# Loading k and v of a packed attention stage as four tokens to a partition, with the last 64 tokens of every head loaded apart

## The chip, the cores and the metric

The kernel runs on one core of one Trainium2 chip. The metric is the time of one execution on the device in microseconds. Before the change the median of 3 runs is 1391.37 us (1388.29 to 1396.19).

## What is computed

The reference is a packed attention followed by two gated feed-forward layers, all in float32:

```python
q, k, v: (8, 8, 576, 64)      # batch, heads, tokens, head_dim
p:       (8, 8, 32, 64)       # 32 packed queries per head

def sm_attn(qq, kk, vv):
    s = (1 / sqrt(64)) * qq @ kk.T
    a = exp(s - max(s)); a = a / (sum(a) + 1e-9)
    return a @ vv

P   = sm_attn(p, k, v)        # 32 x 64 per head, from 576 tokens
out = sm_attn(q, P, P)        # 576 x 64 per head, from 32 packed rows
x   = out as (4608, 512)
x   = (silu(x @ w_gate) * (x @ w_val)) @ w_out
x   = ((x @ w1) * (x @ w2)) @ w3 @ w_out2
```

The change concerns only the first line, the product of the packed queries p with k and v. The order of the 576 tokens is free there, as long as k's scores and v's rows use the same one: max, sum and the weighted sum run over all of them.

## The kernel before

**Units and steps.** The work on p, k and v goes in 16 units, one for each half batch entry (4 heads of 576 tokens); `u = 2 * b + Q`. A loop over steps `s` runs the units as a pipeline. In step `s` the program has, in this order: `pa_kT(s)` (turn k of unit s), the loads of v for unit s and of k for unit s + 4, `pa_s(s - 1)` (scores), `pa_PT(s - 4)` (turn the finished packed rows), `pa_T(s - 2)` (turn the attention weights), `pa_exp(s - 1)`, and `pa_P(s - 3)` (weights times v). Between them, at written-out steps and quarter steps, stand other tasks (`run(s, ...)`): the work on q for the first two batch entries (tables `QS`, `QD`), loads of raw weights (`RAW0`), their conversion on ACT and DVE (`WS`), and the first products of the feed-forward layer (`CS`, `S1`). Each engine takes its instructions in the order of the program text (`manual_schedule`). Behind the pipeline the feed-forward layers follow, which keep the tensor engine busy to the end of the kernel.

**Loads.** All loads stand in one queue, SP's. A unit has 576 KB of k and as much of v. `load_kv` issues for k one DMA into `km` (128 partitions, 18 tokens of one head in each, 4608 bytes in a row), and for v two DMAs into `vm` (96 partitions, 6 tokens of each of 4 heads: 1024 bytes in a row in the first DMA, 512 in the second). `km` and `vm` have four buffers each.

**Waits of the queue.** Every DMA waits for the eighth one ahead of it to land, since the program has eight semaphores for this queue in turn. A load of `km` for unit u also waits until `pa_kT(u - 4)` has read its buffer.

**The unit's work.** `pa_kT` turns p's tile (one PE transpose) and `km` (nine) into PSUM tiles `pkr` and `pk`, and ACT copies them to `kT` in two copies (L501, L502). `pa_s` has 8 matmuls of 64 rows by 32 columns into `psp`; DVE takes the maximum (L517, L518), ACT the exponential with its sum (L524). `pa_T` makes six transposes of 96 columns into `pat` (L536), and ACT copies them to `apT` (L540). `pa_P` has 24 matmuls of 96 rows by 32 columns and 64 moving columns (L550), accumulated over six groups of tokens, and DVE divides by the sum (L554).

**What the prediction's steps touch:** `load_p` L466, `load_kv` L472, `pa_kT` L489, `pa_s` L505, `pa_T` L530, `pa_P` L543, and the step loop at L604. The conversion of raw weights is `conv` at L332; its ACT part is L345, and stands in ACT's queue ahead of that step's copies.

Of the kernel before, what the change touches and what calls it, by code (L numbers as in the profile page):

```python
# [8 lines left out]
F32 = mybir.dt.float32  # L9
# [3 lines left out]
AF = mybir.ActivationFunctionType  # L13
# [4 lines left out]
KVB = 4  # L18
VB = 4
# [19 lines left out]
def packed_attention_moe_kernel(  # L39
# [24 lines left out]
    nc = tc.nc  # L64
    B, H, S, D = q.shape
# [3 lines left out]
    DF2 = w1.shape[1]  # L69
    HS = S // 2  # L70
    NR = S // 32
    NV = 6
    PK = S // NV
    NF = DFF // 128
    NB32 = S // 32
    ND = DM // 128
# [4 lines left out]
    scale = 1.0 / float(D) ** 0.5  # L81

    def pool(name, side, bufs=1, **kw):
        return tc.alloc_tile_pool(name=name, bufs=bufs, side=side, reuse_waits="tile", **kw)
# [21 lines left out]
    ident = const.tile([128, 128], F32, name="ident")  # L106
# [354 lines left out]
    pa = pool("pa", "left", bufs=2)  # L461

    kv = {}
    zp = pa.tile([128, B, 2, 2, 64], F32, tag="zp", name="zp", bufs=1)

    def load_p(b0, b1):  # L466
        nc.sync.dma_start(zp[:, b0:b1, :, 0], p[b0:b1].rearrange("b (q h) j d -> (h j) b q d", q=2))

    def twice_p(b0, b1):
        nc.gpsimd.tensor_copy(zp[:, b0:b1, :, 1], zp[:, b0:b1, :, 0])  # L470

    def load_kv(u, nm):  # L472
        if not 0 <= u < 2 * B:
            return
        b, Q = divmod(u, 2)
        src = {"k": k, "v": v}[nm]
        if nm == "k":
            m = pa.tile([128, NR, D], F32, tag="km", name=f"km{u}", bufs=KVB)
            nc.sync.dma_start(m, src[b, 4 * Q:4 * Q + 4].rearrange("h (p r) d -> (h p) r d", r=NR))
        else:  # L480
            m = pa.tile([PK, 4, NV, D], F32, tag="vm", name=f"vm{u}", bufs=VB)
            rows = src[b, 4 * Q:4 * Q + 4].rearrange("h (p r) d -> p h r d", r=NV)
            for r0, r1 in ((0, 4), (4, NV)):
                pin_at["sp"] = nc.sync.dma_start(m[:, :, r0:r1], rows[:, :, r0:r1])
        kv[nm, u] = m

    kT_t, ap_t, apT_t, sm_t, Pd_t = {}, {}, {}, {}, {}

    def pa_kT(u):  # L489
        km = kv.pop(("k", u))  # L490

        kT = pa.tile([128, NR // 2 + 1, 128], F32, tag="kT", name=f"kT{u}")
        b, Q = divmod(u, 2)
        t1 = psum1(f"pkr{u}")
        nc.tensor.transpose(t1[:, 128:256], zp[:, b, Q].rearrange("p e d -> p (e d)"), ident)
        t = psum(f"pk{u}")
        for m in range(NR // 2):
            nc.tensor.transpose(
                t[:, m // 4, 128 * (m % 4):128 * (m % 4) + 128] if m < 8 else t1[:, 0:128],
                km[:, 2 * m:2 * m + 2, :].rearrange("p r d -> p (r d)"), ident)  # L500
        nc.scalar.copy(kT[:, 0:8], t.rearrange("p a (m n) -> p (a m) n", n=128))  # L501
        nc.scalar.copy(kT[:, 8:10], t1[:, 0:256].rearrange("p (m n) -> p m n", n=128))  # L502
        kT_t[u] = kT

    def pa_s(u):  # L505


        kT = kT_t.pop(u)
        t = psum(f"psp{u}")
        for hq in range(4):  # L510
            for e in range(2):
                es = slice(64 * e, 64 * e + 64)
                nc.tensor.matmul(
                    t[hs[hq], e, 0:HS].rearrange("j (m p g) -> j g m p", m=3, g=3), lhsT=kT[es, 9, hs[hq]],
                    rhs=kT[es, 0:9, hs[hq]].rearrange("d (g m) p -> d g m p", g=3), start=True, stop=True, tile_position=(64 * e, 32 * hq))
        mx = pa.tile([128, 1], F32, tag="mx", name=f"mx{u}")
        nc.vector.reduce_max(mx, t[:, :, 0:HS], axis=AX.XY)  # L517
        nc.vector.tensor_scalar_mul(mx, mx, -scale)  # L518
        return t, mx

    def pa_exp(u, t, mx):
        a = pa.tile([128, NV, PK], F32, tag="ap", name=f"ap{u}")
        sm = pa.tile([128, 1], F32, tag="sm", name=f"sm{u}", bufs=3)
        nc.scalar.activation(  # L524
            a.rearrange("j (m e) p -> j e m p", e=2),
            t[:, :, 0:HS].rearrange("j e (m p) -> j e m p", p=PK),
            AF.Exp, bias=mx, scale=scale, accum_out=sm)
        ap_t[u], sm_t[u] = a, sm

    def pa_T(u):  # L530
        a, sm = ap_t.pop(u), sm_t[u]
        nc.vector.tensor_scalar(sm, sm, 1e-9, None, op0=ALU.add)
        nc.vector.reciprocal(sm, sm)
        t = psum(f"pat{u}")
        for r in range(NV):
            nc.tensor.transpose(  # L536
                t[:PK, r % 2, 128 * (r // 2):128 * (r // 2) + 128],
                a[:, r], ident)
        aT = pa.tile([PK, 2, 3, 128], F32, tag="apT", name=f"apT{u}")
        pin_at["act"] = nc.scalar.copy(aT, t[:PK, :, 0:384].rearrange("p e (m n) -> p e m n", m=3))  # L540
        apT_t[u] = aT

    def pa_P(u):  # L543
        vm = kv.pop(("v", u))
        aT = apT_t.pop(u)
        sm = sm_t.pop(u)
        t = psum1(f"pP{u}")
        for r in range(NV):
            for hq in range(4):
                nc.tensor.matmul(  # L550
                    t[hs[hq], 0:64], lhsT=aT[:, r % 2, r // 2, hs[hq]], rhs=vm[:, hq, r, :],
                    start=(r == 0), stop=(r == NV - 1), tile_position=(0, 32 * hq))
        Pd = pa.tile([128, 2, 64], F32, tag="Pd", name=f"Pd{u}")
        pin_at["dve"] = nc.vector.tensor_scalar(  # L554
            Pd, t[:, 0:64].rearrange("p (o d) -> p o d", o=1).to_broadcast([128, 2, 64]), sm, None, op0=ALU.mult)
        Pd_t[u] = Pd

    def pa_PT(u):
        t = psum1(f"pPT{u}")[:, 0:128]
        nc.tensor.transpose(t, Pd_t.pop(u).rearrange("p a b -> p (a b)"), ident)  # L560
        nc.scalar.copy(PTd[:, u], t)  # L561

    U = 2 * B
    load_p(0, 1)
# [32 lines left out]
    def run(s, slot):  # L597
        for at in [at for at in extra if s + slot <= at < s + slot + 0.25]:
            for fn, args in extra.pop(at):
                fn(*args)  # L600

    last = int(max(max(extra), U + 3))
    with tc.manual_schedule(engines=M0):
        for s in range(last + 1):  # L604
            if s < U:
                pa_kT(s)
            load_kv(s - VD, "v")
            load_kv(s + KVB, "k")
            run(s, 0)
            run(s, 0.25)  # L610
            if 0 <= s - 1 < U:
                x = pa_s(s - 1)
            if 0 <= s - 4 < U:
                pa_PT(s - 4)
            run(s, 0.5)
            if 0 <= s - 2 < U:
                pa_T(s - 2)
            if 0 <= s - 1 < U:
                pa_exp(s - 1, *x)
            if 0 <= s - 3 < U:  # L620
                pa_P(s - 3)
            run(s, 0.75)
# [466 lines left out]
```

## Time and profile before

| | |
|---|---|
| time, median of 3 runs | 1391.37 us (1388.29 to 1396.19) |
| span of the profiled execution | 1393.5 us (the profile gives no other time for it) |
| PE busy | 1351.7 us, 97% of the span |
| PE weight loads, DVE, ACT, POOL busy | 1240.4, 656.0, 574.4, 384.4 us |
| chain that ended last | PE 80% of the span |
| DMA queue of SP | 228.64 MB in 188752 packets, 55.2% of 16 DMA engines |
| granted TensorE clock, mean | 0.993 |

The profile is of one execution, and its 1393.5 us stand 2.1 us above the median of the runs and inside their spread. Busy shares over the whole span say little about the change, which lies in the first tenth of the kernel: the prediction reads the stretches there one by one. [...]

### The profile page before, as it was taken

The page shows a single profiled execution, that of the slowest core. Times are in us where ns is not written, and L with a number is a line of the kernel's source. Part 1 is how long each engine was busy: PE and PEld are TensorE (multiplying, and loading weights), DVE is VectorE, ACT ScalarE, POOL GpSimd, SP SyncE. Part 2 cuts the span into 40 slices and gives each one's busy share as a digit, 9 for nine tenths or more (in the row PEclk, how much of TensorE's full clock was granted, in tenths as well). Part 3 has the DMA queues.
Part 4 walks back from the last instruction along what each step waited for, and adds up shares of the span by engine and source line. Part 5 has one row for each costly group of instructions (what it writes and reads, how often), then busy time and mean ns, then how long its engine had stood idle before and what let it go on. Part 6 is the DMA issues. An engine that isn't in the chain of part 4 may idle for free.

```text
span 1393.5 us, 25570 instructions
## 1 busy us (share of the span) xinstructions
PE 1351.7 (97%) x10228; PEld 1240.4 (89%) x10228; DVE 656.0 (47%) x946; ACT 574.4 (41%) x940; POOL 384.4 (28%) x309
## 2 busy tenths in 40 slices
PE   7779999999999999999999989999999999999998
PEld 5558899999999999999888989989999899898997
DVE  3466668436464365553263377833423323234130
ACT  5575635336243463344554245533323233333231
POOL 0223223333323332253444225502112022021120
PEclk9899999999999999999999999999999999999999
DMA  9997667544355544135452148937638357285441
GB/s 272 251 236 200 217 189 240 169 120 107 117 127 169 159 122 142 51 117 159 125 151 87 61 132 289 330 112 223 193 115 253 131 175 237 70 251 174 133 155 46
DMA packets 188870, 230.27 MB, mean 165 GB/s; under 512 B 70736, under 2 KB 119888, under 8 KB 188752
## 3 DMA queue, kind: packets, MB, share of 16 engines
q1 hardware_dynamic: 188752, 228.64, 55.2%
q8 instruction: 81, 1.33, 0.4%
q14 instruction: 37, 0.30, 0.1%
HBM read 179.04 MB, written 49.55 MB: 164 GB/s over the span
## 4 chain that ended last, share of the span: by engine, by line
PE 80%; DVE 2%; POOL 2%; DMA 1%; issue 1%; ACT 1%; SPq 0%; DVEq 0%; POOLq 0%; ACTq 0%
PE px L653 19%; PE pA L962 14%; PE po L1026 14%; PE pg L440 9%; PE pv L440 8%; PE pB L962 7%; PE pC L962 3%; PE pc L408 3%; PE pw L717 2%; PE psq L205 1%; POOL ul L88 0%; DMA wo3r<-wo3d 0%; POOL wo2l L88 0%; DMA x2r<-X2d 0%; DVE x2T L787 0%
## 5 line engine op out<-in xcount | busy, mean ns | idle before, releaser
L88 POOL TENSOR_TENSOR ul<-u,uh 128x576 fp32r<-128x576 f32 x96 | 146.0, 1521 | 333.2 <-ACT uh L92 328.2
L982 POOL TENSOR_TENSOR c<-s,s 128x384 f32<-128x384 f32 x48 | 49.6, 1033 | 378.9 <-ACT s L977 378.1
L653 PE MATMUL px<-uh,woh 128*128 128x384 f32 x576 | 147.9, 337 | 2.4 <-DVE acc L663 1.4
L653 PE MATMUL px<-ul,woh 128*128 128x384 f32 x576 | 147.2, 336 | 2.6 <-POOL ul L88 2.6
L653 PE MATMUL px<-uh,wol 128*128 128x384 f32 x576 | 147.0, 336 | 0.0
L977 ACT COPY s<-pA 128x384 f32<-128x384 f32 x144 | 69.0, 479 | 183.1 <-PE pA L962 178.6
L449 DVE TENSOR_TENSOR u<-u,pv 128x576 f32<-128x576 f32 x96 | 71.8, 749 | 109.9 <-PE pv L440 96.9
L1026 PE MATMUL po<-wo_hi,abh 128*128 128x512 f32 x288 | 112.2, 389 | 1.0 <-ACT abh L92 1.0
L1026 PE MATMUL po<-wo_hi,abl 128*128 128x512 f32 x288 | 112.3, 390 | 0.3 <-DVE abl L88 0.3
L1026 PE MATMUL po<-wo_lo,abh 128*128 128x512 f32 x288 | 112.2, 389 | 0.0
L92 ACT CAST uh<-u 128x576 fp32r<-128x576 f32 x96 | 64.7, 674 | 115.2 <-DVE u L449 114.8
L663 DVE TENSOR_TENSOR acc<-acc,px 128x768 f32<-128x768 f32 x72 | 68.1, 948 | 92.2 <-PE px L653 92.0
L653 PEld LDWEIGHTS px<-uh,woh 128*128 128x128 f32 x576 | 103.4, 189 | 5.3 <-DVE acc L663 1.8
L653 PEld LDWEIGHTS px<-ul,woh 128*128 128x128 f32 x576 | 104.5, 188 | 3.1 <-POOL ul L88 3.1
L653 PEld LDWEIGHTS px<-uh,wol 128*128 128x128 f32 x576 | 104.6, 189 | 0.0
L88 DVE TENSOR_TENSOR abl<-ab,abh 128x768 fp32r<-128x768 f32 x48 | 47.0, 980 | 104.5 <-ACT abh L92 104.4
L88 POOL TENSOR_TENSOR wol<-wof,woh 128x512 fp32r<-128x512 f32 x48 | 63.4, 1334 | 107.3 <-ACT woh L92 101.3
L440 PE MATMUL pg<-aTh,ch 128*128 128x288 f32 x384 | 87.1, 308 | 1.2 <-ACT u L445 1.2
L445 ACT ACTIVATE u<-pg 128x576 f32<-128x576 f32 x96 | 62.4, 651 | 59.8 <-PE pg L440 58.2
L440 PE MATMUL pv<-aTh,ch 128*128 128x288 f32 x384 | 82.9, 297 | 2.2 <-ACT PTd L561 1.5
L440 PE MATMUL pg<-aTh,cl 128*128 128x288 f32 x384 | 82.4, 296 | 0.0
L440 PE MATMUL pv<-aTl,ch 128*128 128x288 f32 x384 | 82.1, 295 | 0.0
(305 smaller groups left out, 3107.1 us busy)
## 6 DMA issues: line engine op xcount, KB each, us to landing
ws<-wsd SPq DMA_DIRECT2D x245, 256.0 KB, 3.1
wf<-Wd SPq DMA_DIRECT2D x36, 512.0 KB, 5.0
wsd<-ws SPq DMA_DIRECT2D x49, 256.0 KB, 3.0
km<-in_k_dram SPq DMA_DIRECT2D x16, 576.0 KB, 13.3
wof<-wod SPq DMA_DIRECT2D x36, 256.0 KB, 3.0
x2r<-X2d SPq DMA_DIRECT2D x24, 384.0 KB, 5.3
out_dram<-o SPq DMA_DIRECT2D x36, 256.0 KB, 2.0
raw_w<-in_moe_w_dram SPq DMA_DIRECT2D x16, 512.0 KB, 4.3
```

The lines of the kernel that those rows point to most:

```text
L88: return eng.tensor_tensor(out=out, in0=src, in1=hi.bitcast(F32), op=ALU.subtract)
L92: nc.scalar.copy(hi, src)
L408: nc.tensor.matmul(t[hs[at], b, Q], lhsT=PTd[es, 2 * (2 * P + b) + Q, hs[hq]], rhs=w[es, 2 * Q + hq // 2].rearrange("p g n -> p (g n)"), s ...
L440: nc.tensor.matmul(t[:, hf, 0:HS], lhsT=w[:, b % 2, Q, cols], rhs=x[:, Q, hf, :], start=first, stop=last,)
L445: x = nc.scalar.activation(u, t[:, :, 0:HS], AF.Silu)
L449: x = nc.vector.tensor_tensor(out=u, in0=u, in1=t[:, :, 0:HS], op=ALU.mult)
L653: nc.tensor.matmul(t[:, h, 0:CW], lhsT=w[:, 128 * d:128 * d + 128], rhs=x[:, CW * c:CW * c + CW], start=first, stop=last,)
L663: nc.vector.tensor_tensor(out=o, in0=o, in1=t[:, :, 0:CW], op=ALU.add)
L962: nc.tensor.matmul(bk[n], lhsT=w[:, hl, 128 * d:128 * d + 128], rhs=r[:, d], start=(first and d == 0 and i == 0), stop=(d == 1 and i == 2) ...
L977: nc.scalar.copy(o, t)
L982: on.tensor_tensor(out=r, in0=o, in1=t, op=op)
L1026: nc.tensor.matmul(t, lhsT=a[:, j, cols], rhs=w[:, f], start=first, stop=last)
```

## The change

The 576 tokens of a head are cut into 512 and 64. The first 512 of k and of v are loaded in one DMA for each unit and tensor, as four tokens to each of 128 partitions: 1024 bytes in a row for each of 4 heads. The last 64 tokens of all units go into two tiles `rest["k"]` and `rest["v"]` (`kr` and `vr` in the lists below): head hq of a unit takes the 32 partitions 32 hq to 32 hq + 31, two tokens in each, 512 bytes in a row. `load_rest(u0, u1, nm)` issues four DMAs, one for each group of 32 partitions: units 0 to 3 ahead of the first k and, for v, ahead of the third k; units 4 to 15 in step 1, eight DMAs in a row, ahead of k of unit 5.

`pa_kT` turns the unit's part of `rest["k"]` in place of the ninth slice of `km`, and ACT makes three copies where it made two. `pa_s` reads and writes its 288 columns in order. `pa_exp` writes in order. `pa_T` has four transposes of 128 columns in place of six of 96, and DVE turns the weights of the last 64 tokens in 32x32 blocks (`apR`). `pa_P` has 16 matmuls of 128 rows and 8 of 32 rows on the diagonal 32x32 parts of the array, all summed into the same PSUM rows.

```diff
+    rest = {nm: pa.tile([128, 2 * B, 2 * D], F32, tag=f"{nm}r", name=f"{nm}r", bufs=1) for nm in "kv"}
+    def load_rest(u0, u1, nm):
+        src = {"k": k, "v": v}[nm]
+        for hq in range(4):
+            nc.sync.dma_start(
+                rest[nm][hs[hq], u0:u1],
+                src[u0 // 2:u1 // 2, :, TM:S].rearrange(
+                    "b (q h) (p r) d -> h p (b q) (r d)", h=4, r=2)[hq])
...
     def load_kv(u, nm):
-            nc.sync.dma_start(m, src[b, 4 * Q:4 * Q + 4].rearrange("h (p r) d -> (h p) r d", r=NR))
...
-            for r0, r1 in ((0, 4), (4, NV)):
-                pin_at["sp"] = nc.sync.dma_start(m[:, :, r0:r1], rows[:, :, r0:r1])
+        m = pa.tile([128, 4, NV * D], F32, tag=f"{nm}m", name=f"{nm}m{u}", bufs={"k": KVB, "v": VB}[nm])
+        x = nc.sync.dma_start(m, src[b, 4 * Q:4 * Q + 4, 0:TM].rearrange("h (p r) d -> p h (r d)", r=NV))
...
     def pa_kT(u):
+        nc.tensor.transpose(t1[:, 0:128], rest["k"][:, u], ident)
+        for m in range(8):
...
-        nc.scalar.copy(kT[:, 0:8], t.rearrange("p a (m n) -> p (a m) n", n=128))
-        nc.scalar.copy(kT[:, 8:10], t1[:, 0:256].rearrange("p (m n) -> p m n", n=128))
+        nc.scalar.copy(by_head[:, :, 0:256], t.rearrange("p a (h n) -> p (a h) n", n=256))
+        nc.scalar.copy(by_head[:, :, 256:HS], t1[:, 0:128].rearrange("p (h n) -> p h n", n=32))
+        nc.scalar.copy(kT[:, 4 * HS:4 * HS + 128], t1[:, 128:256])
...
     def pa_T(u):
+        nc.vector.transpose(out=aR, in_=a[:, :, 256:HS])
...
         for r in range(NV):        # NV: 6 before, 4 now
             nc.tensor.transpose(
-                t[:PK, r % 2, 128 * (r // 2):128 * (r // 2) + 128],
-                a[:, r], ident)
+                t[:, 128 * r:128 * r + 128], a[:, r % 2, 128 * (r // 2):128 * (r // 2) + 128], ident)
...
     def pa_P(u):
+        for r in range(2):
+            for hq in range(4):
+                nc.tensor.matmul(
+                    t[hs[hq], 0:64], lhsT=aR[hs[hq], r], rhs=rest["v"][hs[hq], u, D * r:D * r + D],
+                    start=False, stop=(r == 1), tile_position=(32 * hq, 32 * hq))
...
     load_p(0, 1)
+    load_rest(0, 4, "k")
     load_kv(0, "k")
     load_kv(1, "k")
     load_p(1, 3)
+    load_rest(0, 4, "v")
     load_kv(2, "k")
...
             load_kv(s - VD, "v")
+            if s == 1:
+                load_rest(4, U, "k")
+                load_rest(4, U, "v")
             load_kv(s + KVB, "k")
```

SP's queue at the start of the program, ahead of the first step, stood thus before (`zp` is p, `km0` is k of unit 0):

```order
L467 DMA zp_105<-in_p_dram 128x2x64
L479 DMA km0_107<-in_k_dram 128x1152
L479 DMA km1_109<-in_k_dram 128x1152
L467 DMA zp_105<-in_p_dram 128x4x64
L479 DMA km2_112<-in_k_dram 128x1152
```

and now:

```order
L468 DMA zp_105<-in_p_dram 128x2x64
L478 DMA kr_106<-in_k_dram 32x4x128 x4
L489 DMA km0_113<-in_k_dram 128x4x256
L489 DMA km1_115<-in_k_dram 128x4x256
L468 DMA zp_105<-in_p_dram 128x4x64
L478 DMA vr_107<-in_v_dram 32x4x128 x4
L489 DMA km2_122<-in_k_dram 128x4x256
```

Four small loads now stand ahead of k of unit 0, and four more ahead of k of unit 2.

SP's queue from k of unit 3 to k of unit 6, that is the loads of steps 0 to 2 (`qr` are rows of q), before:

```order
L479 DMA km3_118<-in_k_dram 128x1152
L484 DMA vm0_137<-in_v_dram 96x4x256
L484 DMA vm0_137<-in_v_dram 96x4x128
L479 DMA km4_140<-in_k_dram 128x1152
L164 DMA qr0_0_142<-in_q_dram 128x1152
L484 DMA vm1_159<-in_v_dram 96x4x256
L484 DMA vm1_159<-in_v_dram 96x4x128
L479 DMA km5_162<-in_k_dram 128x1152
L164 DMA qr0_1_164<-in_q_dram 128x1152
L484 DMA vm2_196<-in_v_dram 96x4x256
L484 DMA vm2_196<-in_v_dram 96x4x128
L479 DMA km6_199<-in_k_dram 128x1152
```

and now:

```order
L489 DMA km3_128<-in_k_dram 128x4x256
L489 DMA vm0_148<-in_v_dram 128x4x256
L489 DMA km4_150<-in_k_dram 128x4x256
L165 DMA qr0_0_152<-in_q_dram 128x1152
L489 DMA vm1_170<-in_v_dram 128x4x256
L478 DMA kr_106<-in_k_dram 32x12x128 x4
L478 DMA vr_107<-in_v_dram 32x12x128 x4
L489 DMA km5_180<-in_k_dram 128x4x256
L165 DMA qr0_1_182<-in_q_dram 128x1152
L489 DMA vm2_215<-in_v_dram 128x4x256
L489 DMA km6_217<-in_k_dram 128x4x256
```

The eight loads of the rest of units 4 to 15 now stand ahead of k of unit 5 and all that follows it; v of a unit is one DMA and no longer two.

PE in one step without other tasks, step 8 (`psp7` are unit 7's scores, `pat6` unit 6's weights, `pP5` unit 5's packed rows), before:

```order
L495 MATMUL pkr8_674<-ident_66,zp_105 128x128
L498 MATMUL pk8_676<-ident_66,km8_318 128x128 x8
L498 MATMUL pkr8_674<-ident_66,km8_318 128x128
L513 MATMUL psp7_698<-kT7_588 32x3x96 x8
L560 MATMUL pPT4_710<-ident_66,Pd4_669 128x128
L536 MATMUL pat6_715<-ident_66,ap6_641 96x128 x6
L550 MATMUL pP5_727<-vm5_405,apT5_639 32x64 x24
```

and now, in step 7, which has the same parts:

```order
L503 MATMUL pkr7_607<-ident_66,zp_105 128x128
L505 MATMUL pkr7_607<-ident_66,kr_106 128x128
L507 MATMUL pk7_609<-ident_66,km7_263 128x128 x8
L523 MATMUL psp6_633<-kT6_512 32x288 x8
L573 MATMUL pPT3_645<-ident_66,Pd3_603 128x128
L545 MATMUL pat5_652<-ident_66,ap5_575 128x128 x4
L558 MATMUL pP4_662<-vm4_334,apT4_573 32x64 x16
L563 MATMUL pP4_662<-vr_107,apR4_564 32x64 x8
```

Two transposes fewer, the transpose of the rest ahead of those of `km`, and the last eight matmuls on other parts of the array.

## Rows read from the trace of the kernel before

**Rows 1.** Windows: four stretches of the span, all engines. After each stretch its length:

```profile
core 0: us, PE busy (x) PEld busy (x) DVE busy (x) ACT busy (x) POOL busy (x), PEclk, DMA share, GB/s
0.00:22.04 22.04, 16.60 (x239) 12.46 (x239) 6.00 (x17) 12.29 (x22) 2.11 (x9) 1.00 0.97 285
22.04:99.04 77.00, 58.05 (x1044) 42.09 (x1038) 39.04 (x101) 45.12 (x83) 15.11 (x12) 0.91 1.09 243
99.04:175.00 75.96, 70.55 (x773) 62.34 (x773) 51.62 (x77) 47.62 (x73) 23.08 (x16) 1.00 0.71 213
175.00:1393.50 1218.50, 1206.51 (x8180) 1123.55 (x8180) 559.37 (x752) 469.39 (x765) 344.06 (x273) 1.00 0.51 155
```

**Rows 2.** Windows of PE for steps 5, 6, 7, 10, 12, 13, 15; columns as the header above, PE alone:

```profile
22.04:30.24 8.20, 5.66 (x112) 1.00 1.12 256
30.24:34.67 4.43, 4.28 (x103) 1.00 1.10 233
34.67:40.27 5.60, 3.96 (x87) 1.00 1.10 239
...
53.30:64.69 11.39, 6.17 (x113) 0.83 1.09 250
...
70.74:75.99 5.25, 4.14 (x81) 1.00 1.09 245
75.99:83.01 7.02, 4.84 (x120) 1.00 1.11 246
...
90.77:99.04 8.27, 5.89 (x93) 1.00 1.03 223
```

**Rows 3.** Waits from 22.04 to 99.04 us: waiter, awaited, us, times, longest:

```profile
ACT wf L345 <- DMA raw_w<-in_moe_w_gate_dram: 9.9, 2, 6.5
...
ACT wf L345 <- DMA raw_w<-in_moe_w_val_dram: 4.4, 2, 2.8
...
PE pP L550 <- ACT PTd L561: 3.8, 1, 3.8
```

**Rows 4.** DMA packets in four windows: 4.2 to 6.2, 11.3 to 12.3, 131.2 to 134, 145.2 to 146.2:

```profile
DMA packets 257, 0.73 MB, mean 365 GB/s; under 512 B 103, under 2 KB 103, under 8 KB 257
...
DMA packets 229, 0.23 MB, mean 227 GB/s; under 512 B 10, under 2 KB 226, under 8 KB 229
...
DMA packets 3002, 0.37 MB, mean 134 GB/s; under 512 B 3002, under 2 KB 3002, under 8 KB 3002
...
DMA packets 372, 0.40 MB, mean 397 GB/s; under 512 B 10, under 2 KB 362, under 8 KB 372
```

**Rows 5.** Timeline of SP's queue: start, duration, issue:

```profile
0.74 0.44 SPq L467 DMA_DIRECT2D zp<-in_p_dram  x1
1.24 0.93 SPq L479 DMA_DIRECT2D km<-in_k_dram  x2
...
9.78 1.18 SPq L484 DMA_DIRECT2D vm<-in_v_dram  x2
```

**Rows 6.** Timeline of PE: first transposes of k, begin of step 4, k of unit 5:

```profile
5.35 1.97 PE L498 MATMUL pk<-ident,km 128*128 128x128 f32 x8 [1.74 <-DMA km<-in_k_dram]
...
16.65 0.33 PE L495 MATMUL pkr<-ident,zp 128*128 128x128 f32 x1
...
23.12 1.06 PE L498 MATMUL pk<-ident,km 128*128 128x128 f32 x8 [0.76 <-DMA km<-in_k_dram]
```

**Rows 7.** Groups by line and shape, 0 to 230 us: busy us, mean ns | idle before:

```profile
L540 ACT COPY apT<-pat 96x768 f32<-96x768 f32 x16 | 13.0, 816 | 4.0 <-PE pat L536 4.0
...
L92 ACT CAST woh<-wof 128x512 fp32r<-128x512 f32 x9 | 5.6, 621 | 10.5 <-DVE wof L349 10.5
...
L502 ACT COPY kT<-pkr 128x256 f32<-128x256 f32 x16 | 6.1, 381 | 0.0
...
L212 DVE STREAM_TRANSPOSE sT<-psq 128x288 f32<-128x288 f32 x8 | 3.5, 462 | 0.3 <-PE psq L205 0.3
```

**Rows 8.** Timeline of ACT: a change of its function table in step 15:

```profile
93.26 1.28 ACT L445 ACT_TABLE_LOAD   x1
```

More of the change, by code (lines that the diff above doesn't have):

```diff
@@ L71, in packed_attention_moe_kernel @@
     NR = S // 32
-    NV = 6
-    PK = S // NV
+    TR = 64
+    TM = S - TR
+    NV = TM // 128
     NF = DFF // 128
@@ L476, in load_kv @@
         src = {"k": k, "v": v}[nm]
-        if nm == "k":
-            m = pa.tile([128, NR, D], F32, tag="km", name=f"km{u}", bufs=KVB)
-            nc.sync.dma_start(m, src[b, 4 * Q:4 * Q + 4].rearrange("h (p r) d -> (h p) r d", r=NR))
-        else:
-            m = pa.tile([PK, 4, NV, D], F32, tag="vm", name=f"vm{u}", bufs=VB)
-            rows = src[b, 4 * Q:4 * Q + 4].rearrange("h (p r) d -> p h r d", r=NV)
-            for r0, r1 in ((0, 4), (4, NV)):
-                pin_at["sp"] = nc.sync.dma_start(m[:, :, r0:r1], rows[:, :, r0:r1])
+        m = pa.tile([128, 4, NV * D], F32, tag=f"{nm}m", name=f"{nm}m{u}", bufs={"k": KVB, "v": VB}[nm])
+        x = nc.sync.dma_start(m, src[b, 4 * Q:4 * Q + 4, 0:TM].rearrange("h (p r) d -> p h (r d)", r=NV))
+        if nm == "v":
+            pin_at["sp"] = x
         kv[nm, u] = m
@@ L490, in pa_kT @@
         km = kv.pop(("k", u))
-        kT = pa.tile([128, NR // 2 + 1, 128], F32, tag="kT", name=f"kT{u}")
+        kT = pa.tile([128, 4 * HS + 128], F32, tag="kT", name=f"kT{u}")
+        by_head = kT[:, 0:4 * HS].rearrange("d (h s) -> d h s", h=4)
         b, Q = divmod(u, 2)
@@ L496, in pa_kT @@
         t = psum(f"pk{u}")
-        for m in range(NR // 2):
+        nc.tensor.transpose(t1[:, 0:128], rest["k"][:, u], ident)
+        for m in range(8):
             nc.tensor.transpose(
-                t[:, m // 4, 128 * (m % 4):128 * (m % 4) + 128] if m < 8 else t1[:, 0:128],
-                km[:, 2 * m:2 * m + 2, :].rearrange("p r d -> p (r d)"), ident)
-        nc.scalar.copy(kT[:, 0:8], t.rearrange("p a (m n) -> p (a m) n", n=128))
-        nc.scalar.copy(kT[:, 8:10], t1[:, 0:256].rearrange("p (m n) -> p m n", n=128))
+                t[:, m // 4, 128 * (m % 4):128 * (m % 4) + 128],
+                km[:, m // 2, 128 * (m % 2):128 * (m % 2) + 128], ident)
+        nc.scalar.copy(by_head[:, :, 0:256], t.rearrange("p a (h n) -> p (a h) n", n=256))
+        nc.scalar.copy(by_head[:, :, 256:HS], t1[:, 0:128].rearrange("p (h n) -> p h n", n=32))
+        nc.scalar.copy(kT[:, 4 * HS:4 * HS + 128], t1[:, 128:256])
         kT_t[u] = kT
@@ L513, in pa_s @@
                 nc.tensor.matmul(
-                    t[hs[hq], e, 0:HS].rearrange("j (m p g) -> j g m p", m=3, g=3), lhsT=kT[es, 9, hs[hq]],
-                    rhs=kT[es, 0:9, hs[hq]].rearrange("d (g m) p -> d g m p", g=3), start=True, stop=True, tile_position=(64 * e, 32 * hq))
+                    t[hs[hq], e, 0:HS], lhsT=kT[es, 4 * HS + 32 * hq:4 * HS + 32 * hq + 32],
+                    rhs=kT[es, HS * hq:HS * hq + HS], start=True, stop=True, tile_position=(64 * e, 32 * hq))
         mx = pa.tile([128, 1], F32, tag="mx", name=f"mx{u}")
@@ L521, in pa_exp @@
     def pa_exp(u, t, mx):
-        a = pa.tile([128, NV, PK], F32, tag="ap", name=f"ap{u}")
+        a = pa.tile([128, 2, HS], F32, tag="ap", name=f"ap{u}")
         sm = pa.tile([128, 1], F32, tag="sm", name=f"sm{u}", bufs=3)
[L524 to L527, printed above, removed]
+        nc.scalar.activation(a, t[:, :, 0:HS], AF.Exp, bias=mx, scale=scale, accum_out=sm)
         ap_t[u], sm_t[u] = a, sm
@@ L531, in pa_T @@
         a, sm = ap_t.pop(u), sm_t[u]
+        aR = pa.tile([128, 2, 32], F32, tag="apR", name=f"apR{u}")
+        nc.vector.transpose(out=aR, in_=a[:, :, 256:HS])
         nc.vector.tensor_scalar(sm, sm, 1e-9, None, op0=ALU.add)
         nc.vector.reciprocal(sm, sm)
-        t = psum(f"pat{u}")
+        t = psum(f"pat{u}")[:, 0]
         for r in range(NV):
             nc.tensor.transpose(
-                t[:PK, r % 2, 128 * (r // 2):128 * (r // 2) + 128],
-                a[:, r], ident)
-        aT = pa.tile([PK, 2, 3, 128], F32, tag="apT", name=f"apT{u}")
-        pin_at["act"] = nc.scalar.copy(aT, t[:PK, :, 0:384].rearrange("p e (m n) -> p e m n", m=3))
-        apT_t[u] = aT
+                t[:, 128 * r:128 * r + 128], a[:, r % 2, 128 * (r // 2):128 * (r // 2) + 128], ident)
+        aT = pa.tile([128, NV, 128], F32, tag="apT", name=f"apT{u}")
+        pin_at["act"] = nc.scalar.copy(aT, t.rearrange("p (r n) -> p r n", r=NV))
+        apT_t[u] = aT, aR
     def pa_P(u):
         vm = kv.pop(("v", u))
-        aT = apT_t.pop(u)
+        aT, aR = apT_t.pop(u)
         sm = sm_t.pop(u)
@@ L550, in pa_P @@
                 nc.tensor.matmul(
-                    t[hs[hq], 0:64], lhsT=aT[:, r % 2, r // 2, hs[hq]], rhs=vm[:, hq, r, :],
-                    start=(r == 0), stop=(r == NV - 1), tile_position=(0, 32 * hq))
+                    t[hs[hq], 0:64], lhsT=aT[:, r, hs[hq]], rhs=vm[:, hq, D * r:D * r + D],
+                    start=(r == 0), stop=False, tile_position=(0, 32 * hq))
+        for r in range(2):
[3 more added lines that the diff above has]
+                    start=False, stop=(r == 1), tile_position=(32 * hq, 32 * hq))
         Pd = pa.tile([128, 2, 64], F32, tag="Pd", name=f"Pd{u}")
```

## The prediction

> **What bounds the kernel now.** I read the windows first. Behind 175 us PE is busy 1206.51 of 1218.50 us, and from 99.04 to 175 for 70.55 of 75.96 [rows 1]: there PE itself is the bound, and whatever comes earlier moves it as a whole. Ahead of it lie the steps of k and v. From 22.04 us (step 5) to 99.04 us (start of step 16) PE is busy only 58.05 of 77.00 us while the DMA engines' mean busy share is 1.09 [rows 1]: transfers bound this stretch. The waits say how they reach PE. Little is put down to km itself (0.76 us at unit 5 [rows 6]); most goes through ACT, which stands 9.9 and 4.4 us before the conversion of a raw weight that hasn't landed, with its copies for PE queued behind it, so that PE waits 3.8 us at once for ACT's `PTd` [rows 3]. PE's clock also falls: 0.83 of full in step 10, where the longest of those waits lies, and 0.91 over the stretch [rows 1, 2].
>
> The DMA windows say why transfers are slow at a share of 1.09. With k in flight (4608 bytes in a row, 128 partitions; 154 of the 257 packets) they move 365 GB/s; with v in flight (1024 and 512 bytes, 96 partitions) 227; with raw weights (1024 bytes in a row, 128 partitions, the third kind) 397; with q's later loads (128 bytes in a row, 32 partitions) 134 [rows 4]. The third against the second is the heart of the case: pieces of 1024 bytes aren't slow as such, so v's slowness goes with its 96 partitions or its 512-byte half.
>
> **The transfers.** A load of k or v falls from 0.590 to 0.524 MB, since each unit's last 64 tokens (0.066 MB for k, as much for v) go into the rests. For the new form (1024 bytes, 128 partitions) the nearest row is 397 GB/s, the far one v's 227; I take 350, a little under k's own 365, since k's neighbours in the queue aren't all of this form: 1.5 us for a load. k and v now take 0.590/365 + 0.590/227 = 1.6 + 2.6 = 4.2 us for a unit at these rates; the new pair takes 3.0 without its rest.
>
> The rests are 16 DMAs into 32 partitions each, with 512 bytes in a row. No row shows that form. Bounds: 134 GB/s (same partitions, smaller pieces) and 397. I take 200, nearest to v's 227, which has part of its pieces this small and more partitions. Units 0 to 3 of k or of v: 0.262 MB, 1.3 us; units 4 to 15: 0.786 MB, 3.9 us each for k and v.
>
> [...]
>
> **The start: slower.** Four issues at 0.44 us [rows 5] now stand ahead of the first k, 1.8 us, so its landing moves from 5.35 [rows 6] to 7.1. From there the queue in the order of the list, at the rates above: km1 8.6, p 9.0 (0.13 MB, at the 285 GB/s of rows 1), rest of v 10.3, km2 11.8, p 12.9, km3 14.4, vm0 15.9, km4 17.4, q 19.0 (0.590 MB at 365), vm1 20.5, rest of k 24.4, rest of v 28.3, km5 29.8. Issuing doesn't bind: a pair for v with 768 rows takes 1.18 us [rows 5], eight loads of 384 rows some 5, beside 7.8 us of transfer. Step 4 needs the rest of k: its transposes of km start at about 24.4 where the step began at 16.65 [rows 6]. PE has by then stood for some 5 us and starts at the lower clock, for which I add 1 us to the 5.4 us of the step (16.65 to 22.04). Step 5 begins at 30.8 in place of 22.04: **8.8 us later**. What waits in SP behind the eight loads is km5, q, vm2 and km6; the first of them is due at 30.8 and lands at 29.8.
>
> **Steps 5 to 15: faster.** With transfers out of the way a step lasts as long as PE's work, at full clock: 4.0 us without other tasks (3.96 and 4.14 in steps 7 and 12), 4.3 with q's scores (step 6), 5.7 with q's transposes too (step 5), 4.8 with the first product (step 13), 5.9 with the half feed-forward stage (step 15) [rows 2]. For 5 to 15: 5.7, 4.3, 4.0, 4.0, 5.4 (transposes alone), 5.7, 4.3, 4.0, 4.8, 5.9, 5.9, together 54.0. Idle time that isn't a transfer's: 0.15 for each step (4.43 less 4.28), 1.7; in step 15 the 2.4 us by which its span passes PE's work, with a table load of 1.28 us of ACT [rows 2, 8], 0.15 of it counted already; 1.1 in step 12, kept likewise. Sum about **58.8 against 77.0, 18.2 less**. Do the transfers allow that? From q behind km5 to the raw weights that step 15 needs, 10 loads of k, 14 of v, 5 raw weights at 0.524 MB and 3 of q: 17.0 MB, 48.5 us at 350. They do as long as the mean rate stays above 289 GB/s.
>
> **Small parts.** [...] ACT: the copy of `apT` goes from 816 ns to about 621 (a 128x512 copy), the split copy of `kT` costs 381 more at most (a second copy like the first) and nothing at least; between 0.2 less and 0.2 more for a unit, ACT being busy 45.12 of 77.00 us. DVE: 16 transposes of 64 columns, under 462 ns each (288 columns) and over nothing, at most 7.4 us beside 38 us of idle time [rows 1, 7]. I put all of these at nothing; if ACT or PE were short, they would cost up to 3 us either way.
>
> **Sum.** 8.8 − 18.2 = −9.4 us on a profiled span of 1393.5, so 1384.1; the span stands 2.1 above the median of 1391.4, so **1382**. Behind step 16 PE bounds as before and the shift is carried to the end.
>
> **Rivals.**
> *The start eats the gain* (0.27). Rests at 134 GB/s: 11.7 us in place of 7.8, plus 0.7 for each of the two early ones, 5.2 in all; and a step may keep 0.4 us of waits for ACT that the transfers hide now, 4 us over eleven. For it: no row shows the form of the rests, and step 4 waits for all four of k's. Against: ACT is busy only 45.12 of 77.00 us in these steps [rows 1]. It gives 1385 to 1391.
> *Pieces, not partitions* (0.08): 1024-byte pieces of k and v, unlike the weights', move at v's 227 whatever the partitions. Each load takes 2.3 us and not 1.5, the eight up to km5 make 6 us more there (step 5 at about 37), and 17.0 MB then take 75 us: step 16 starts near 112 in place of 99, **slower by 13, 1404**. It decides from the point where the mean rate falls under about 250 GB/s. Against it: 397 GB/s for weights.
> *More than I count* (0.12): rests at 300 or better and steps without the idle time kept above, 2.6 + 3 + 1 us more: 1375.
> *Moved, not won* (0.05): ACT or the weights' loads behind 99 us take it back, so that step 16 is early and 175 us isn't. Against: PE's 70.55 of 75.96. It gives 1388 to 1392.
>
> **How the numbers follow.** Forecast 0.48, at 1382, within 1379 to 1386. A difference of 0.5%, 7 us, is about what a measurement of this kernel can tell from no change. Faster than 1384.4: 0.42 of the forecast's 0.48, all 0.12 of the larger gain, 0.01 of the rest, **0.55**. Slower than 1398.3: 0.08 and some of unknown cause, **0.10**. The remainder, **0.35**. The range 1373 to 1392 leaves out the slower case and a little on either side.
>
> **What would show it.** In the profile after: the transposes of km in step 4 near 24 us, step 5 near 31, step 16 near 90; over 340 GB/s where only k, v and weights of the new form are in flight; ACT's waits for raw weights gone; PE's clock nearer 1.0 from step 6 on; one DMA for v in place of two. Wrong would be: step 5 later than 36 us, a mean rate from step 5 to 15 that stays under 250 GB/s with a busy share over 1, or step 16 early and 175 us not.

## The result, and the profile after

The changed kernel takes 1381.62 us (median of 4 runs, 1380.55 to 1382.37), the kernel before 1392.18 beside it (1388.29 to 1396.19). The ratio is 0.9914, 95% interval 0.9886 to 0.9941: **10.6 us faster**, where 9.4 were forecast (1382, within 1373 to 1392). The profiled execution took 1382.37 us, with a span of 1380.6.

Windows of the profile after, all engines. The first two rows cover the same parts of the work as those of [rows 1], to step 5 and steps 5 to 15; the other two go from step 16 to 179 us and from there on:

```profile
core 0: us, PE busy (x) PEld busy (x) DVE busy (x) ACT busy (x) POOL busy (x), PEclk, DMA share, GB/s
0.00:32.72 32.72, 18.22 (x233) 13.24 (x233) 6.17 (x19) 11.99 (x27) 2.12 (x9) 0.90 1.02 258
32.72:90.90 58.18, 51.82 (x1023) 37.23 (x1017) 42.96 (x115) 44.23 (x94) 15.38 (x12) 0.97 0.99 321
90.90:179.00 88.10, 85.99 (x901) 78.00 (x901) 61.68 (x94) 53.28 (x83) 29.68 (x21) 1.00 0.73 214
179.00:1380.00 1201.00, 1190.73 (x8050) 1108.61 (x8048) 547.57 (x736) 463.02 (x754) 338.73 (x268) 1.00 0.49 153
```

The first row is 10.68 us longer than before (22.04), the second 18.82 shorter (77.00). In the second row PE is busy 51.82 of 58.18 us in place of 58.05 of 77.00, and the DMA engines move 321 GB/s in place of 243 at a *lower* share (0.99 against 1.09): a DMA engine that is busy isn't one that moves much, and only the two columns together show it.

The steps that answer to [rows 2] (steps 5, 6, 7, 10, 12, 13, 15), same columns:

```profile
32.72:38.64 5.92, 5.28 (x111) 3.85 (x105) 3.26 (x9) 2.98 (x7) 0.00 (x0) 1.00 1.09 348
38.64:42.65 4.01, 4.01 (x102) 2.85 (x96) 3.30 (x14) 3.19 (x8) 1.16 (x1) 1.00 1.09 348
42.65:46.40 3.75, 3.60 (x86) 2.55 (x80) 3.48 (x11) 3.38 (x9) 2.05 (x2) 1.00 1.07 370
...
56.05:61.90 5.85, 5.24 (x110) 3.86 (x105) 4.04 (x11) 5.03 (x11) 2.33 (x2) 1.00 1.09 350
...
68.36:73.16 4.80, 4.65 (x83) 3.45 (x80) 4.01 (x15) 3.75 (x9) 2.32 (x2) 0.77 1.07 341
73.16:77.86 4.70, 4.70 (x118) 3.06 (x112) 3.71 (x11) 3.84 (x10) 1.16 (x1) 1.00 0.85 279
...
84.54:90.90 6.36, 5.63 (x94) 4.15 (x92) 4.96 (x14) 6.31 (x12) 1.52 (x2) 1.00 0.98 329
```

Step 10, 11.39 us before, lasts 5.85. PE has work for 89% of steps 5 to 15 now, and in the first of them the DMA engines are still busy throughout (1.09), but at 341 to 370 GB/s: they run ahead of PE and no longer hold it up.

DMA windows of the profile after: first the bandwidth of each microsecond from 0 to 40, then the packets from 40 to 80 us:

```profile
GB/s 0 23 108 153 92 263 385 356 270 240 305 293 236 321 348 346 351 401 376 358 298 184 203 191 200 190 200 193 213 345 375 373 355 350 348 362 334 347 346 350
...
DMA packets 12315, 13.23 MB, mean 331 GB/s; under 512 B 401, under 2 KB 12050, under 8 KB 12306
```

The eight slices from 21 to 29 us at 184 to 213 GB/s hold 1.57 MB, as much as the rests of units 4 to 15 have. Behind them, from 29 to 40 us, where k and v of the new form fly, it is 334 to 375.

Timeline of SP's queue and of PE around step 4, with step 0's and step 5's begin; columns: start, duration, what, and the idle time before it with what ended it:

```profile
13.30 5.01 SPq L478 DMA_DIRECT2D kr<-in_k_dram  x4
18.36 6.06 SPq L478 DMA_DIRECT2D vr<-in_v_dram  x4
24.51 0.81 SPq L489 DMA_DIRECT2D km<-in_k_dram  x1
```

```profile
7.30 1.97 PE L507 MATMUL pk<-ident,km 128*128 128x128 f32 x8 [1.81 <-DMA km<-in_k_dram]
...
18.68 0.33 PE L503 MATMUL pkr<-ident,zp 128*128 128x128 f32 x1
26.90 0.45 PE L505 MATMUL pkr<-ident,kr 128*128 128x128 f32 x1 [7.89 <-DMA kr<-in_k_dram]
27.14 1.92 PE L507 MATMUL pk<-ident,km 128*128 128x128 f32 x8
...
32.72 0.33 PE L503 MATMUL pkr<-ident,zp 128*128 128x128 f32 x1
```

Here the price of the change is to be seen: PE stands 7.89 us in step 4, because the first transpose of the step wants `kr` of unit 4, which landed as one of the eight rests. The transposes behind it then run at a granted clock of 0.50 (27.14 to 29.06 us: eight in 1.92 us; in step 5, at 1.00, in 1.04).

In steps 5 to 15 (waits of PE and of ACT, 32.72 to 90.90 us) no entry names a transfer any more; ACT's 9.9 and 4.4 us for raw weights [rows 3] are gone, and so is PE's 3.8 for `PTd`. The largest that are left:

```profile
PE psp L523 <- ACT ap L534: 1.6, 1, 1.6
PE pat L545 <- DVE qT L176: 1.3, 2, 0.6
```

```profile
ACT kT L510 <- PE pk L507: 5.2, 8, 2.1
ACT ap L534 <- DVE mx L528: 5.1, 6, 2.8
```

The small parts, as groups by line and shape from 0 to 230 us (busy us, mean ns | idle before), beside [rows 7]:

```profile
L548 ACT COPY apT<-pat 128x512 f32<-128x512 f32 x16 | 9.9, 620 | 2.2 <-PE pat L545 2.2
L563 PE MATMUL pP<-vr,apR 32*32 32x64 f32 x256 | 7.0, 226 | 0.0
...
L512 ACT COPY kT<-pkr 128x128 f32<-128x128 f32 x16 | 4.6, 288 | 0.0
L511 ACT COPY kT<-pkr 128x128 f32<-128x128 f32 x16 | 4.4, 276 | 0.0
L540 DVE STREAM_TRANSPOSE apR<-ap 128x64 f32<-128x64 f32 x16 | 3.8, 234 | 0.0
```

`apT`'s copy went from 816 ns to 620, where 621 was taken from a copy of the same shape. `kT`'s second copy of 381 became two of 276 and 288: 183 more, so for a unit ACT pays 13 ns less. DVE's transpose takes 234 ns, and PE waits for none of the sixteen. For `kT`'s last copy PE waits 1.0 us in steps 5 to 15, about as before (the kernel before, then the changed one):

```profile
PE pP L550 <- ACT kT L502: 1.2, 2, 0.9
```

```profile
PE pP L558 <- ACT kT L512: 1.0, 4, 0.6
```

On ACT and DVE, then, putting these parts at nothing was right. What PE gains by them shows only where the clock is the same (see the runs without v below).

### The profile page after: what moved, and what is told of

Its sections match the earlier page's. It is cut to its first block, busy times and chain, and to the rows that moved or that the text cites. A ratio compares the mean times of both kernels' runs of the same rounds, so it can differ in the third digit from the quotient of the medians.

```text
span 1380.6 us, 25551 instructions
## 1 busy us (share of the span) xinstructions
PE 1346.8 (98%) x10196; PEld 1237.1 (90%) x10196; DVE 658.4 (48%) x962; ACT 572.5 (41%) x956; POOL 385.9 (28%) x309
## 4 chain that ended last, share of the span: by engine, by line
PE 82%; DVE 2%; POOL 1%; DMA 1%; issue 1%; ACT 1%; SPq 0%; DVEq 0%; POOLq 0%; ACTq 0%
PE px L671 20%; PE pA L980 14%; PE po L1044 14%; PE pg L441 9%; PE pv L441 9%; PE pB L980 7%; PE pC L980 4%; PE pc L409 3%; PE pw L735 2%; PE psq L206 1%; POOL ul L89 0%; POOL wo2l L89 0%; DMA wo3r<-wo3d 0%; DMA x2r<-X2d 0%; DVE x2T L805 0%
```

## The experiments

Five questions: is it partitions or pieces; is it one DMA's partitions or all that fly; did the transfers bind before; do they bind now; and can the start's price be lowered. Each run stands beside runs of the kernel before on the same chip, and the ratios are formed with these; the runs were made on three chips, where the kernel before took 1396.62, 1392.26 and 1391.27 us, so that a difference of a few us from the 1381.62 of the change can also be one between chips. One profiled execution lies up to 4 us from the median of its kernel (in before_without_v it was the shortest of four, in after_without_v the longest), so total times are read from medians, and from a trace only where in the span time goes.

### Pieces or partitions: k_v_two_dmas, k_v_512_bytes, v_96_and_32

Control, two DMAs for each load, over the heads (1024-byte pieces, 128 partitions):

```diff
-        x = nc.sync.dma_start(m, src[b, 4 * Q:4 * Q + 4, 0:TM].rearrange("h (p r) d -> p h (r d)", r=NV))
+        rows = src[b, 4 * Q:4 * Q + 4, 0:TM].rearrange("h (p r) d -> p h (r d)", r=NV)
+        for h in (0, 2):
+            x = nc.sync.dma_start(m[:, h:h + 2], rows[:, h:h + 2])
```

> Control for the two kernels that double the number of DMAs: the changed kernel, each load of k or v as two DMAs of two heads each, over 128 partitions in 1024-byte pieces. Both theories: the same rate; more issues, and eight DMAs in flight hold half the bytes: 1381 to 1385 us.

Measured: 1380.95 us, ratio 0.990 (0.987 to 0.993), at the lower end of what was expected. A second DMA for each load costs nothing that shows.

Half the piece, same partitions:

```diff
+        rows = src[b, 4 * Q:4 * Q + 4, 0:TM].rearrange("h (e p r) d -> e p h (r d)", e=2, r=2)
+        for e in range(2):
+            x = nc.sync.dma_start(m[:, :, 128 * e:128 * e + 128], rows[e])
```

> The changed kernel, each load of k or v as two DMAs over all 128 partitions with pieces of 512 bytes. Theory (partitions): such pieces still move at 300 GB/s or more, at most 0.25 us more for a load, which the idle time of the steps takes in part: 1381 to 1388 us. Rival (pieces): 512-byte pieces go at 200 to 230 GB/s, 0.8 us more for each of 32 loads, 15 to 22 us later: 1396 to 1404 us.

Measured: 1383.27 us, ratio 0.992 (0.989 to 0.995).

Same piece, v alone cut by partitions:

```diff
+        rows = src[b, 4 * Q:4 * Q + 4, 0:TM].rearrange("h (p r) d -> p h (r d)", r=NV)
+        for p0, p1 in ((0, 96), (96, 128)) if nm == "v" else ((0, 128),):
+            x = nc.sync.dma_start(m[p0:p1], rows[p0:p1])
```

> The changed kernel, v of each unit loaded in two DMAs, partitions 0 to 95 and 96 to 127, with the same 1024-byte pieces. Theory (partitions): the 96 partitions were what held v at 227 GB/s in the kernel before; 0.39 MB at about 227 and 0.13 MB at about 195 take 2.4 us in place of 1.5, and as the transfers fill the time up to 72 us, step 16 moves 8 to 12 us later: 1389 to 1394 us. Rival (pieces): the size of the pieces sets the rate, nothing changes but one more issue for a unit: 1381 to 1383 us.

Measured: 1404.33 us, ratio 1.008 (1.005 to 1.011): the gain is gone and more. DMA windows from 40 to 80 us: the control, 512-byte pieces, and the cut at partition 96:

```profile
DMA packets 12972, 13.61 MB, mean 340 GB/s; under 512 B 693, under 2 KB 12707, under 8 KB 12963
```

```profile
DMA packets 20486, 12.18 MB, mean 304 GB/s; under 512 B 640, under 2 KB 20221, under 8 KB 20477
```

```profile
DMA packets 9351, 10.17 MB, mean 254 GB/s; under 512 B 415, under 2 KB 9087, under 8 KB 9343
```

Pieces of 512 bytes cost a tenth of the rate (304 against 340), which these steps can spare: they take 55.9 us (37.15 to 93.06) against the control's 56.6 (33.26 to 89.88), and what this kernel loses lies in the start. Fewer partitions with *unchanged* pieces cost a quarter (254), which they can't, as the window of v_96_and_32 shows:

```profile
34.20:103.25 69.05, 53.70 (x1023) 36.41 (x1017) 40.60 (x115) 44.16 (x94) 15.23 (x12) 0.98 1.10 244
```

ACT's waits for raw weights are back:

```profile
ACT wf L346 <- DMA raw_w<-in_moe_w_gate_dram: 7.1, 2, 6.1
...
ACT wf L346 <- DMA raw_w<-in_moe_w_val_dram: 4.0, 2, 2.3
```

That is the wait of the kernel before, produced at will. The theory of partitions holds, but its price was expected at 7 to 12 us over the change and measured near 23 (23.4 over the control, on the same chip).

No run loads 96 partitions alone: in v_96_and_32 a quarter of v goes in DMAs of 32. For 96 alone the trace of the kernel before has a stretch, from 11.8 to 12.3 us, where every packet is at most 2 KB and nearly all are v's 1024-byte pieces (k's are 4608 bytes long, and 198 GB/s over half a us in 108 packets is a mean of about 920):

```profile
DMA packets 108, 0.10 MB, mean 198 GB/s; under 512 B 4, under 2 KB 108, under 8 KB 108
```

So v was slow in its 1024-byte half already.

### One DMA's partitions: v_halves

```diff
-        for p0, p1 in ((0, 96), (96, 128)) if nm == "v" else ((0, 128),):
+        for p0, p1 in ((0, 64), (64, 128)) if nm == "v" else ((0, 128),):
```

> The changed kernel, with each load of v as two DMAs over 64 partitions each (0 to 63, 64 to 127) in place of one over 128; pieces of 1024 bytes and the whole work stay. In v_96_and_32 the same cut at partition 96 took 1404, about 22 us over the change, and 7 to 12 were expected. Two theories of that price. A DMA's rate goes with the number of its partitions, whatever flies beside it: 64 partitions then move at about half of 350 GB/s, as 32 moved at 184 to 213 in the rests; 14 loads of v, 7.3 MB, at 175 to 230 take 32 to 42 us in place of 21, so step 16 comes 9 to 20 us later than the change's 90.9 and the time is 1390 to 1401. The cut at 96 alone is dear (an uneven cut, whose small part holds a place among the eight DMAs in flight): even halves then cost little, the mean rate from 40 to 80 us stays over 310 GB/s and the time is 1381 to 1386.

Measured: 1409.22 us, ratio 1.012 (1.007 to 1.016), slower still. Windows of steps 5 to 15:

```profile
34.99:105.16 70.17, 55.28 (x1024) 37.92 (x1017) 40.62 (x115) 44.11 (x94) 15.27 (x12) 0.98 1.12 240
```

The idea that the cut at 96 alone is dear falls. Two halves that lie in the queue one behind the other don't add up to the rate of one DMA over all 128 partitions: 240 GB/s at a share of 1.12. Step 16 comes 14.3 us later than in the change, inside the 9 to 20 expected; the time came out 8 us above its range, because the expectation ended at step 16. Behind it another 7.1 us are lost before the first product of `px` (the product with `w_out`), which starts 21.4 us later (144.9 against 123.5): the granted clock of that stretch is 0.91 in place of 1.00, and PE waits 3.1 us for ACT's `uh`. What makes `uh` late wasn't found.

As an estimate by the expectation's lower rate, 175 GB/s for 64 partitions (half of the 350 for 128), a half of 0.262 MB takes 1.5 us, as long as a whole load at 350. If the two halves of a load then run one after the other, 14 loads of v add 14 × 1.5 = 21 us to the 48.5 us that the prediction worked out for these steps' transfers: 69.5. The trace shows 70.17 and so agrees; that the halves run in series is inferred from this sum alone.

### Did the transfers bind before, and do they now: before_without_v, after_without_v

The loads of v for units 4 to 15 are left out; those units use the tiles of units 0 to 3 again, so all work of the engines stays, though the result is another. In the kernel before (in the changed one likewise):

```diff
+            if u >= VB:
+                kv[nm, u] = kept[u % VB]
+                return
+            kept[u] = m = pa.tile([PK, 4, NV, D], F32, tag="vm", name=f"vm{u}", bufs=VB)
```

> The kernel before, with the loads of v of units 4 to 15 left out (these units use the tiles of units 0 to 3): 7.1 MB fewer between 22 and 99 us, all else in place. Theory (transfers bound the steps before): steps 5 to 15 fall from 77 us to the 59 that PE's work takes, 1370 to 1377 us. Rival (the order of ACT and PE bounds them, and the change won through shorter work): 1386 us or more.

Measured: 1378.01 us, ratio 0.990 (0.987 to 0.992), 14 us less than the kernel before, and 1 us above the range of the theory. Windows of its steps 5 to 15:

```profile
21.91:81.99 60.08, 51.80 (x1045) 37.81 (x1039) 41.76 (x103) 44.87 (x83) 15.25 (x12) 1.00 0.83 253
```

60.1 us in place of 77.0, with nothing changed but transfers: they did bind.

> The changed kernel with the same loads of v left out, the rests of v kept. Theory (with 350 GB/s the steps are already bound by PE's work): steps 5 to 15 stay within 4 us of their 58.2, 1377 to 1381 us. Rival (transfers still bind, the busy share is 1.0 up to 72 us): 6 us or more less, 1375 us or below.

Measured: 1382.62 us, ratio 0.994 (0.992 to 0.996), no gain over the change: 1.6 us above the range of the theory, and far from the rival's. Its steps 5 to 15:

```profile
34.69:91.37 56.68, 50.00 (x1022) 35.95 (x1016) 43.22 (x114) 44.00 (x94) 15.37 (x12) 1.00 0.78 236
```

Without most of v they last 56.7 us, with it 58.2, and in k_v_two_dmas, with all of v too, 56.6. So transfers no longer bind there, and a faster load of v is worth 1.5 us at most; what is left is PE's work and its waits for ACT and DVE.

The two runs without v also part the transfers from the shorter work of the new form. Both have PE at a granted clock of 1.00: the old form takes 60.1 us with 51.80 of PE busy, the new one 56.7 with 50.00. Of the 18.8 us that steps 5 to 15 win, by these single executions, about 17 are the transfers' and some 2 the work's. What the change still pays is the start: step 5 at 32.7, against 21.9 in before_without_v.

### The start: rests_by_four, rests_apart, rests_spread

The rests in smaller portions, four units at a time:

```diff
-            if s == 1:
-                load_rest(4, U, "k")
-                load_rest(4, U, "v")
+            if s in (1, 5, 9):
+                load_rest(s + 3, s + 7, "k")
+                load_rest(s + 3, s + 7, "v")
```

> The changed kernel, the rests of units 4 to 15 loaded four units at a time in steps 1, 5 and 9. Theory (the eight early loads cost the start): 1.05 of 1.57 MB, 5.4 us at 195 GB/s, leave the queue ahead of k of unit 5; the transposes of step 4 start near 24 in place of 27.1 us and step 5 near 28 in place of 32.7; part comes back later, where the queue is full to 72 us: 1376 to 1380 us. Rival (transfers bind up to step 16): the bytes are the same, step 16 stays at 91 us: 1381 to 1383 us.

Measured: 1384.84 us, ratio 0.993 (0.990 to 0.995). Both theories missed the time, though step 16 stays near 91 us (90.40), as the rival had it. DMA windows from 40 to 80 us, bandwidth of each microsecond:

```profile
GB/s 168 63 31 98 150 393 402 335 366 353 400 391 376 342 347 353 347 345 346 354 347 349 263 208 102 46 77 89 348 384 362 352 355 346 347 349 358 343 350 351
```

The holes at 40 to 45 and 64 to 68 us are the groups of eight DMAs of 64 KB each. Eight is also how many fly at once in this queue (in the traces of the change and of the kernel before, at most seven others haven't landed yet when a DMA is issued): once the eight are small ones, no large load is in flight beside them, and the rate falls to between 31 and 102 GB/s in seven of these nine slices. The number of DMAs alone doesn't do it: the eight of the change, 192 KB each, keep 184 to 213 GB/s. What the start gets back (step 5 at 30.41 in place of 32.72) is nearly gone by step 16, 0.5 us ahead of the change. The first product of `px` comes 1.9 us later (125.38), behind a stretch with a granted clock of 0.95 in place of 1.00; why, no run shows.

So the next one never puts eight in a row: k's portions in steps 1, 5, 9 and v's in 2, 6, 10; the first rests stand behind the first and the third k; the rest's transpose stands behind `km`'s, to do something while the rest flies. Against the change, in part:

```diff
     load_p(0, 1)
+    load_kv(0, "k")
     load_rest(0, 4, "k")
-    load_kv(0, "k")
...
-            if s == 1:
-                load_rest(4, U, "k")
-                load_rest(4, U, "v")
+            if s in (1, 5, 9):
+                load_rest(s + 3, s + 7, "k")
+            if s in (2, 6, 10):
+                load_rest(s + 2, s + 6, "v")
```

> The changed kernel with the rests loaded four units at a time, k's in steps 1, 5 and 9 and v's one step later, so that never more than four small loads stand in a row; the first rests behind the first load of k and behind the third; the transpose of the rest behind those of km. Theory (rests_by_four was lost to the limit of eight DMAs in flight, which eight small ones fill while the engines run dry): with four large loads always in flight the rate stays near 350 GB/s, step 0 starts 1.5 us earlier, the transposes of step 4 come near 23 us and step 5 near 28: 1374 to 1378 us. Rival (the bytes set step 16 anyway): 1381 to 1385 us.

Measured (5 runs): 1379.68 us, ratio 0.991 (0.989 to 0.993). It lies between the two expectations. PE's wait for the rest in step 4 falls from 7.9 us to 4.1, and step 5 begins at 29.08:

```profile
PE pkr L509 <- DMA kr<-in_k_dram: 4.4, 2, 4.1
```

Step 16 begins at 85.22, 5.7 us ahead of the change, so the bytes don't set it: the rival falls. But the profiled execution is the fastest of the five, 2.1 us under their median. The kernel has the lowest median of those that compute everything, about 2 us under the change, but the ranges overlap: that it beats the change isn't established.

The last one keeps only the first portion of k in step 1 and spreads the others as two DMAs for each of steps 2 to 5 (the fourth argument, new here, picks the group of 32 partitions):

```diff
             if s == 1:
-                load_rest(4, U, "k")
-                load_rest(4, U, "v")
+                load_rest(4, 8, "k")
+            if 2 <= s < 6:
+                load_rest(4, U, "v", (s - 2,))
+                load_rest(8, U, "k", (s - 2,))
```

> As rests_apart, but behind the rest of k of units 4 to 7 in step 1 the others come one DMA at a time: in each of steps 2 to 5 one of v's (units 4 to 15, 196 KB) and one of k's (units 8 to 15, 131 KB). Theory (small loads in a row starve the engines): step 4 as in rests_apart, no low stretch later, 1373 to 1377 us, up to 2 us less than rests_apart. Rival (the bytes set step 16 anyway): 1381 to 1385 us.

Measured (7 runs): 1383.91 us, ratio 0.995 (0.993 to 0.997). The theory missed; the time lies in the rival's range, but step 16 moved (94.23 in place of 90.90), so its reason fails as well. Bandwidth from 40 to 80 us:

```profile
GB/s 171 179 206 331 244 154 174 208 233 327 375 363 361 378 372 377 353 348 350 351 350 349 348 350 348 346 346 350 348 345 350 350 343 362 335 350 347 348 350 347
```

Up to 49 us, while rests are in flight beside the large loads, the rate is 154 to 244 GB/s in all slices but one, so spreading doesn't hide them. v's last rest now came too late, and step 7 lasted from 39.52 to 49.87 us: PE stood 2.06 us for `vr`, and 3.35 us for which the profile names nothing:

```profile
45.88 1.01 PE L558 MATMUL pP<-vm,apT 128*32 128x64 f32 x26 [3.35 <-issue]
...
49.31 0.63 PE L563 MATMUL pP<-vr,apR 32*32 32x64 f32 x10 [2.06 <-DMA vr<-in_v_dram]
```

## Why the prediction was right

**The bound.** That transfers bound steps 5 to 15 is shown by before_without_v: 60.1 us without v's loads. The choice between pieces and partitions, "the heart of the case", is shown by four runs with equal work. The rival that pieces set the rate gave 1404 for the change. With 512-byte pieces the kernel still takes 1383; with fewer partitions it does take 1404 to 1409. The trace of the kernel before could have told it ahead: its window of 227 GB/s [rows 4] has 0.23 MB in 229 packets, a mean of about 1000 bytes, so v's 1024-byte pieces fill it and not the 512-byte ones.

**The start: 8.8 us later forecast, 10.7 measured.** The first transposes of `km` come at 7.30 (7.1 forecast). The rate of the rests, 200 taken between 134 and 397, was 184 to 213. Both rests of units 4 to 15, put at 7.8 us together, took about 8 (1.57 MB from 21 to 29 us). The step that was off is the order of landing: the prediction let k's four land at 24.4 and v's after them, but the transposes of step 4 start only at 27.14. SP issues v's from 18.36 us on, and the slices of 21 to 29 us move both; k's last seems to share the time with v's first, though no run isolated this. The lower clock behind the stall, put at 1 us, is in the trace (granted 0.50 and not 1.00, 1.92 against 1.04 us for eight transposes); from these transposes to step 5 it is 5.6 us in place of 6.4.

**Steps 5 to 15: 58.8 us forecast, 58.18 measured.** The total hides two errors that cancel: PE's work was forecast at 54.0 and is 51.82, its idle time at 4.8 and is 6.36. The old form at clock 1.00 took 51.80 already (before_without_v), so the 54.0 were too much for it too; the new one takes 50.00 there (after_without_v), some 2 us less, which the prediction had put at nothing; and the clock takes most of that back. after_without_v confirms that at most 1.5 us of the stretch is the transfers'. Of "PE's clock nearer 1.0 from step 6 on" only the mean is right (0.97 against 0.91). Step 11 has a wait of 1.6 us for ACT's `ap`, and the clock falls behind it; windows of PE (length, busy, clock, DMA share, GB/s):

```profile
64.00:66.00 2.00, 0.57 (x16) 1.00 1.09 347
66.00:68.00 2.00, 2.00 (x55) 0.79 1.10 349
68.00:70.00 2.00, 2.00 (x24) 0.50 1.09 349
70.00:72.00 2.00, 2.00 (x25) 0.86 1.09 349
```

In 68 to 70 us the granted clock is 0.50, and step 12 stretches to 4.80 us.

**Behind step 16: "the shift is carried to the end".** It isn't quite: step 16 is 8.1 us earlier (90.90 against 99.04; 9.4 forecast), the first `px` product 11.1 (123.49 against 134.59), the span 12.9. The stretch from step 16 to that product, before and after:

```profile
99.04:134.59 35.55, 31.64 (x465) 26.21 (x465) 24.02 (x40) 24.50 (x40) 14.16 (x10) 1.00 0.74 201
```

```profile
90.90:123.49 32.59, 30.70 (x461) 25.72 (x461) 23.60 (x43) 23.50 (x40) 14.17 (x10) 1.00 0.74 196
```

PE is idle 1.9 us in place of 3.9, and its wait of 1.5 us for `PTd` is down to 0.4. Behind step 16 ACT waited 1.8 us for raw weights (`wof`) before the change, and not at all after it; that this wait is what made PE's shorter isn't shown. So the prediction missed a small gain of 3.0 us, more than the 1.9 that it missed in the start. Part of the 12.9 is the chosen execution: the medians differ by 10.6.

That 1382 was hit within 0.4 us is in part luck: the forecast of the start was 1.9 us too good, that of steps 5 to 15 was 0.6 too bad, and the 3.0 won behind them weren't in it. The mechanism, transfers that stop binding against a start that gets longer, came out as forecast.

**The rivals.** *The start eats the gain* named the right weak point, but its first part came to 1.9 us and not 5.2, and of its second, 4 us of waits for ACT, the trace has at most 1.6 more idle time than forecast (PE's wait for `ap` in step 11 is of this kind). *Moved, not won* falls, since the first `px` product and the end of the kernel are early too. *More than I count* didn't come about.

## What to carry to other kernels

Read a stretch's DMA share together with its GB/s: here a share over 1 at 240 GB/s went with transfers in a form that bound the steps, and the number of partitions of each single DMA, 128 or fewer, counted for more than 512 or 1024 bytes in a piece (240 and 254 GB/s with v in fewer than 128, 304 with 512-byte pieces over 128). Leaving loads out of a copy of the kernel, with tiles used again, shows in one run whether transfers bind, and how far a better form can help: here down to the 57 to 60 us that the engines' work takes anyway. Read such a run from the same begin to the same end of the work as the kernel that it stands beside. Leftovers that must go into few partitions belong where nothing waits for them yet, in portions that never put eight small ones in a row into a queue of eight: here eight of 64 KB let it fall to between 18 and 102 GB/s.

## What the runs showed of the hardware

- Loads of v cut at partition 64 or 96 cost 28 and 23 us over the change, more than was worked out from the rates of other loads: 240 and 254 GB/s from 40 to 80 us against 340 for two DMAs over all partitions. For 64, steps 5 to 15 agree with an estimate for two loads in series (70.17 us, estimated 69.5); why 96 and 32 take nearly as long (69.1 against 70.2 us) wasn't found.
- The rests, 512-byte pieces in 32 partitions, move at 184 to 213 GB/s; 512-byte pieces over 128 partitions at 304 in the mix.
- With eight DMAs of 64 KB in a row the queue of eight fell to between 18 and 102 GB/s for most of 4 us each time; with eight of 192 KB it kept 184 to 213.
- after_without_v begins step 5 at 34.7 us, 2 us later than the change, though it loads less; this wasn't followed up.
